# An adaLN block with dilated local attention and a token mixer on one core: modulation rows from four column groups, norm statistics on either engine, the gate folded into the mixer, and a new order of operations

## The chip, the cores and the metric

The kernel runs on one NeuronCore of a Trainium2 chip. Five engines work from instruction queues of their own, each in order: TensorE (PE, matrix products into PSUM), VectorE (DVE), ScalarE (ACT, activation functions and evictions of PSUM), GpSimd (POOL) and SyncE (SP, which issues most transfers). The metric is device microseconds of one execution. A profile has a span of its own, from the first to the last instruction, which is a little shorter than the execution's time.

## The reference

The input x has 2048 tokens of 512 values; everything is bfloat16 outside the sums.

```python
mod = (_silu(c) @ w_mod).reshape(1, 6, 1, -1)
sa, ca, ga, sb, cb, gb = (mod[:, i] for i in range(6))
h = _layernorm(x) * (1 + ca) + sa
x = x + ga * A(h)          # 32 heads of 16; key offsets 0, 2, ... 14
h = _layernorm(x) * (1 + cb) + sb
x = x + gb * B(h)

def A(h):                  # dilated local attention
    q, k, v = split(h @ wqkv)
    logits = q . k[pos - off] * 16 ** -0.5, masked where pos < off
    return (softmax(logits) @ v[pos - off]) @ wo

def B(h):                  # mixes tokens, not channels
    h = _layernorm(h)
    u = gelu(einsum('bsd,sf->bdf', h, w1) + b1)     # f = 1792
    return transpose(einsum('bdf,fs->bds', u, w2) + b2)
```

The gate `ga` scales columns of `wo`; `gb` scales columns (channels) of the mixer's result; `b2` belongs to a token, `b1` to a hidden unit f.

## The kernel before

All 16 token tiles of 128 rows stay in `xx` on chip. The attention runs in four chunks of 512 tokens. For each chunk: the statistics of the first norm (`ln1s`, one per tile, by `bn`, L340: a `bn_stats` and a `bn_aggr` on DVE), the reciprocal deviation (`rstd`, L346: on ACT an Ln and then an Exp with scale -0.5), the negated mean (`negmean`, L352), the norm itself (`ln1n`, L356, on either engine), transposes through PE (`tr`), the scale and shift while these are evicted (`hT`, L529), and q, k, v (`qkv`, L560, evicted by `evq`, `evk`, `evv`). Shifted copies of v are made by 16 transfers per chunk (`vd`, L595).

The logits are four products on DVE (`qk`, 128x4096) summed over channels by column-tiled matmuls (`red`); `max` on DVE and `sub` on PE subtract the maximum, `exp` on ACT makes the weights, `sum` on PE adds them, `rb` (L645) takes on ACT the Ln of the sum and the Exp of its negative, `smul` on DVE scales, `a2` and `a2ev` spread the weights, four products `pv` on DVE and `pvacc` on PE make the output, evicted into `o_sb` by `oev` (L691). `wo` (L707) projects it and adds x by an identity matmul. `x1ev` (L709) evicts the new x with its sum, and `x1sq` (L712) takes the sum of squares on ACT. `mv2` (L721) turns both into the variance on DVE; `rstd2`, `nb2`, the norm `t`, the scale and shift by rows on DVE (`aff`), statistics `ln3s`, `rstd3`, `nb3` and the norm `h3` give the mixer's input.

The mixer's first product (`mlp1`, L786) runs over tokens in two levels, tiles 0 to 7 and 8 to 15. A name such as `mlp1_0_31_4` gives the level, the block of 256 hidden units and its half, and the tile at which four matmuls of 512 columns begin. Level 0 is parked in `gT` (`park`), level 1 is added to it (`gadd`, DVE) and passed through `gelu` (ACT). The second product (`mlp2`, L847) makes 16 output tiles of 14 matmuls; `fin` (L854) adds `b2`, multiplies by the gate row `gb_bc` and adds x, in two DVE passes of 128x512; `st_out` stores. The last tile is done in two halves.

The six modulation vectors come from `sc`, the SiLU of c. Two of them are wanted as columns (`modcols`). The other four are wanted as rows on all 128 partitions: `mod_row` (L469) spreads `sc` into 128 equal columns, multiplies by 512 columns of `w_mod` in four matmuls, and evicts the row to `ga_bc`, `sb_bc`, `ab_bc` or `gb_bc`. `gmul` scales `wo` by `ga_bc`.

Each operation is an entry of a graph with its reads and writes. Nothing schedules them: `schedule` (L139) takes the text `ORDER` (L27 to L76) word by word and emits each operation there; a digit after a colon gives its PSUM slot (four slots of two banks), a letter its engine where there are two. Each engine's queue is the order of its operations in that text. SP's transfers stand in the same text and wait in their own queue. `_EngProxy.wrapped` (L174) records every operation, so that the profile shows nearly everything under L175, and groups are told apart by their tiles.

One word of `ORDER` is `act_table` (L407): it loads a set of activation tables on ACT by its number, 6. In the text of before it is the fourth word.

Of the kernel before, what the change touches and what calls it, by code (L numbers as in the profile page):

```python
# [27 lines left out]
consts ld_x00 consts2 act_table ld_c ld_w0 ld_x02 ld_x2 ld_wmodA ld_wmodB ln1s1 cps:0 warm:1 ld_b2 silu_exp ln1s0  # L28
ld_wmod5 halo0 ld_b1 rstd1_0_0 ld_x1 ln1s3 ld_w1 nb1_0_0 ln1s2 ln1n0:a silu_dve ln1n1:a ld_wo2 sc_rep rstd1_0_2 ln1s9
nb1_0_2 ln1s8 ld_x3 ln1n3:v ln1n2:v ln1s11 ld_w2 modcols:2 ln1s10 tr0_10:3 tr0_12 modcols_cp ld_wmod2 rstd1_2_0  # L30
biascols:0 tr0_00:1 hT0_2 tr0_02 biascols_cp modrow5:2 hT0_0 hT0_3 hT0_1 gb:a qkvq0_1:0 ld_wo3 ln1s5 ld_wmod3
qkvq0_0:3 ln1s6 evq0_1:a qkvk0_1:1 ln1s7 evq0_0:a ld_w1_0_3 ln1s4 qkvq0_2:2 evk0_1:a qk0_1 rstd1_1_0 qkvk0_0:0
evq0_2:a qkvk0_2:3 evk0_0:a nb1_1_0 ln1n6:v ln1n7:a ld_wo0 qk0_0 ld_wo1 ln1n4:a qkvv0_0:1 ld_wmod4 ln1n5:a evk0_2:a
ln1s13 tr1_10:2 evv0_0:a tr1_00:0 ln1s12 red0_0:3 hT1_0:a ln1s14 red0_1 khalo1:a qkvv0_2:1 hT1_2:a qk0_3 hT1_3:a
hT1_1:a modrow2:2 evv0_2:a ln1s15 qkvk1_0:0 ga:a vd0_100 qk0_2 vhalo1:a rstd1_3_0 vd0_011 vd0_110 qkvq1_0:1 evk1_0:a
vd0_001 vd0_101 gmul vd0_031 red0_2 evq1_0:a vd0_131 red0_3 nb1_3_0 nb1_2_0 ln1n10:v vd0_000 qkvk1_2:2 ln1n8:a max0
vd0_030 ln1n9:a vd0_010 qk1_0 ln1n11:a vd0_020 qkvq1_2:0 vd0_111 evk1_2:a vd0_121 khalo2:a vd0_130 tr2_10:1 qk1_1
# [15 lines left out]
mlp1_0_31_0 h3_4:a mlp1_0_01_0 qk3_2 h3_5:a vd3_111 vd3_121 mlp1_0_31_4 vd3_131 mlp1_0_00_4 vd3_101 qk3_3 vd3_031
mlp1_0_11_4 mlp1_0_01_4 mlp1_0_10_4 pv2_0 park0_0:a red3_2 park0_1:a red3_3 mlp1_0_30_4 max3 vd3_120 pvacc2_0:0
vd3_110 park0_3:a pvacc2_1 vd3_130 pv2_2 sub3 oev2_1:a vd3_100 mlp1_0_60_0:1 ld_w1_1_5 exp3 mlp1_0_60_4 ld_w1_1_0
pv2_3 sum3 mlp1_0_61_0 rb3 ld_w1_1_4 mlp1_0_61_4 smul3 pvacc2_2:3 park0_6:a a2_3_0:0 ld_w2_4 a2_3_1 pvacc2_3 a2ev3:a
mlp1_0_20_0:2 oev2_3:a pv3_0 mlp1_0_20_4 wo11:1 ld_w1_1_1 wo8:0 pv3_1 x1ev11 x1sq11 pvacc3_0:3 x1ev8 ld_w2_0 wo9:1
x1sq8 pv3_2 pvacc3_1 x1ev9 wo10:0 oev3_1:a mlp1_0_21_0 pv3_3 x1ev10 ld_w1_1_3 mlp1_0_21_4 x1sq10 x1sq9 pvacc3_2:1
ld_w1_1_2 mv2_2_0 pvacc3_3 park0_2:v rstd2_2_0 mlp1_0_40_0:3 oev3_3:a nb2_2_0 mlp1_0_40_4 t8:v ld_w2_3 t11:a t10:v
t9:v wo12:0 aff2_0 wo14:2 x1ev12 x1sq12 wo15:1 ld_w2_6 x1ev14 ln3s2_3 wo13:0 x1sq14 ln3s2_2 x1ev15 mlp1_0_50_0:2  # L60
ln3s2_0 x1ev13 x1sq15 mlp1_0_51_0 ln3s2_1 x1sq13 ld_w2_7 mlp1_0_51_4 mv2_3_2 rstd3_2_0 mv2_3_0 rstd2_3_2 mlp1_0_50_4
nb3_2_0 h3_11:v h3_9:a nb2_3_2 h3_10:v mlp1_0_41_0 t15:v rstd2_3_0 t14:v h3_8:a nb2_3_0 aff3_2 mlp1_0_41_4 t13:a
mlp1_1_00_0:1 ld_w1_1_6 t12:a ln3s3_3 mlp1_1_01_0 park0_5:a aff3_0 ld_w2_1 mlp1_1_40_0:0 park0_4:a mlp1_1_41_0 ln3s3_0
mlp1_1_30_0:2 ln3s3_1 mlp1_1_31_0 ln3s3_2 rstd3_3_0 ld_w2_2 mlp1_1_10_0:3 nb3_3_0 rstd3_3_2 h3_12:v nb3_3_2 h3_13:a
mlp1_1_11_0 h3_14:v h3_15:v mlp1_1_10_4 mlp1_1_31_4 ld_w2_5 mlp1_1_00_4 mlp1_1_40_4 mlp1_1_11_4 mlp1_1_41_4 gadd1
mlp1_1_01_4 gelu3 mlp1_1_20_0:3 gadd0 gelu2 mlp1_1_20_4 gelu0 mlp1_1_21_0 gelu1 mlp1_1_21_4 mlp1_1_30_4 gadd2
mlp1_1_50_0:1 gadd3 gelu5 mlp1_1_51_0 gelu4 mlp1_1_51_4 gelu7 gadd4 mlp1_1_50_4 gelu6 gelu8 mlp1_1_60_0:3 gadd5
# [155 lines left out]
def kernel(  # L223
# [14 lines left out]
    WARM: int = 15,  # L238
# [28 lines left out]
    def bank(s_, h):  # L267
        return ps[s_.i][:, h, :]
# [37 lines left out]
    gb_bc = T([P, D], F32, "gb_bc")  # L306
# [19 lines left out]
    va2 = small([P, TPC], "va2")  # L326
# [13 lines left out]
    def bn(src, s6, mvt, reads, writes, name):  # L340
        def f():
            nc.vector.bn_stats(s6, src)
            nc.vector.bn_aggr(mvt, s6)
        add("dve", 0.82, f, reads=reads, writes=writes, name=name, lat=0.08)

    def rstd(var_ap, lv_t, rs_t, reads, writes, name):  # L346
        def f():
            nc.scalar.activation(lv_t, var_ap, ACT.Ln, bias=epscol[:, 0:1])
            nc.scalar.activation(rs_t, lv_t, ACT.Exp, scale=-0.5)
        add("act", 0.5, f, reads=list(reads) + ["consts"], writes=writes, name=name, lat=0.05)  # L350

# [545 lines left out]
```

## Time and profile before

| | |
|---|---|
| median of 3 executions (lowest, highest) | 209.24 us (209.02, 209.30) |
| the profiled execution's own time | 209.11 us |
| its span | 207.4 us |
| mean granted TensorE clock | 0.99 |
| instructions | 3356 |
| accumulating activations on ACT | 16 into `xx`, 16 into `junk` |
| statistics on DVE (`BATCH_NORM_STATS2`) | 32, 0.67 us each |
| table loads on ACT | 2, 1.28 us each |

The page gives busy time per engine and, in its chain, the work that ended last, followed back from the end. A timeline row has its start, its duration, the engine, the operation, and output and input by the program's tile names. Neighbouring instructions of one engine overlap by about a tenth of a microsecond, so the distance between starts is what one of them costs in a full queue. `lv` is the result of the Ln of `rstd`, `rs` that of its Exp; `lns` and `rb` are the same for the softmax; `ee` is the softmax's exponential; `junk` takes the unused output of a pass that is run for its sum.

### The profile page before, as it was taken

The numbers are of one execution on the slowest core, as the hardware profiler recorded it, in microseconds if no ns is written. First come the engines' busy times: TensorE is split into PE (matmuls) and PEld (weight loads), VectorE is DVE, ScalarE is ACT, GpSimd is POOL, SyncE is SP. The second block draws the span as 40 slices with busy tenths as digits, with TensorE's granted clock in tenths as the row PEclk, the third lists the DMA queues.
The fourth block names the chain that finished last, engine by engine and source line by source line (L and its number), as shares of the span: only waits on it lengthen the run. The fifth ranks groups of instructions, "written<-read, shape, count | busy, mean of one in ns | idle before, by whom it ended". The sixth has DMA issues, their size and how long they took to land.

```text
span 207.4 us, 3356 instructions
## 1 busy us (share of the span) xinstructions
PE 196.4 (95%) x1290; PEld 91.4 (44%) x1290; DVE 158.4 (76%) x211; ACT 118.9 (57%) x220; POOL 4.0 (2%) x27
## 2 busy tenths in 40 slices
PE   5489999999999999999999999999999999999993
PEld 2155544444454445443353344444444444444452
DVE  2878999999999999999987998954544534543553
ACT  2436998989799999985567979752562000000000
POOL 7000000000000000000000000000000000000000
PEclk9969999999999999999999999999999999999999
DMA  6999939995690496099499999999000111011011
GB/s 185 361 326 319 259 99 179 170 222 128 159 157 4 118 253 150 6 254 259 126 211 290 291 293 292 290 290 250 4 0 0 54 51 48 28 51 51 28 51 51
DMA packets 41571, 32.96 MB, mean 159 GB/s; under 512 B 2004, under 2 KB 38996, under 8 KB 41556
## 3 DMA queue, kind: packets, MB, share of 16 engines
q1 hardware_dynamic: 41548, 32.75, 64.1%
q8 instruction: 10, 0.16, 0.4%
q14 instruction: 5, 0.04, 0.1%
q10 hardware_dynamic: 8, 0.00, 0.0%
HBM read 22.03 MB, written 2.10 MB: 116 GB/s over the span
## 4 chain that ended last, share of the span: by engine, by line
PE 74%; ACT 11%; DMA 6%; DVE 4%; issue 3%; ACTq 0%; SPq 0%; DVEq 0%
PE ps L175 74%; DMA b_t<-in_B_b_dram 4%; ACT h L175 2%; DMA w_q<-in_A_wqkv_dram 2%; ACT hTb L175 1%; ACT v_c L175 1%; ACT junk L175 1%; DVE h L175 1%; DVE st L175 1%; ACT xx L175 1%; ACT n_sb L175 1%; DVE n_sb L175 1%; ACT o_sb L175 0%; ACT a2sb L175 0%; ACT q_sb L175 0%
## 5 line engine op out<-in xcount | busy, mean ns | idle before, releaser
L175 DVE TENSOR_TENSOR pvb<-a2sb,vD 128x4096 bf16<-128x4096 bf16 x16 | 35.9, 2288 | 1.9 <-ACT a2sb L175 1.8
L175 DVE TENSOR_TENSOR prod<-q_sb,k_c 128x4096 bf16<-128x4096 bf16 x16 | 36.2, 2282 | 0.8 <-ACT k_c L175 0.8
L175 PE MATMUL ps<-h,wst 128*128 128x512 bf16 x128 | 29.6, 379 | 0.4 <-ACT h L175 0.3
L175 PEld LDWEIGHTS <-wst 128*128 128x128 bf16 x128 | 12.2, 98 | 16.5 <-issue 2.7
L175 PE MATMUL ps<-gT,vD 128*128 128x512 bf16 x84 | 18.3, 379 | 0.0
L175 PE MATMUL ps<-woq,o_sb 128*128 128x512 bf16 x64 | 16.5, 380 | 0.0
L175 DVE SCALAR_TENSOR_TENSOR q_sb<-ps,b2col,gb_bc 128x512 f32<-128x512 f32 x8 | 6.0, 751 | 12.9 <-PE ps L175 12.9
L175 PEld LDWEIGHTS <-vD 128*128 128x128 bf16 x116 | 9.2, 97 | 14.2 <-DMA vD<-in_w_mod_dram 4.3
L175 PE MATMUL ps<-hTb,w_q 128*128 128x512 bf16 x64 | 15.2, 380 | 0.2 <-ACT hTb L175 0.2
L175 PE MATMUL ps<-hTb,w_k 128*128 128x512 bf16 x64 | 15.2, 380 | 0.0
L175 PE MATMUL ps<-hTb,w_v 128*128 128x512 bf16 x64 | 15.1, 379 | 0.0
L175 PEld LDWEIGHTS <-w_q 128*128 128x128 bf16 x96 | 10.2, 109 | 11.1 <-issue 1.7
L175 DVE SCALAR_TENSOR_TENSOR k_c<-ps,b2col,gb_bc 128x512 f32<-128x512 f32 (+1 forms) x9 | 6.2, 692 | 11.4 <-PE ps L175 11.4
L175 PEld LDWEIGHTS <-o_sb 128*128 128x128 bf16 x106 | 10.0, 98 | 10.5 <-issue 1.7
L175 DVE BATCH_NORM_STATS2 st<-xx 128x6 f32<-128x512 bf16 x16 | 10.8, 676 | 4.4 <-DMA xx<-in_A_x_dram 4.4
L175 PEld LDWEIGHTS <-w_k 128*128 128x128 bf16 x80 | 8.7, 111 | 8.9 <-issue 0.8
L175 PE MATMUL ps<-gT,prod 128*128 128x512 bf16 x56 | 12.4, 379 | 0.1
L175 PE MATMUL ps<-gT,pvb 128*128 128x512 bf16 x56 | 12.2, 379 | 0.0
L175 PEld LDWEIGHTS <-w_v 128*128 128x128 bf16 x80 | 8.6, 110 | 7.9 <-issue 0.4
L175 ACT ACTIVATE xx<-ps 128x512 bf16<-128x512 f32 x16 | 9.4, 586 | 2.7 <-PE ps L175 2.5
L175 DVE BATCH_NORM_STATS2 st<-h 128x6 f32<-128x512 bf16 x16 | 10.8, 674 | 0.1
L175 ACT ACTIVATE hTb<-ps,sacol,a1col 128x512 bf16<-128x512 bf16 x14 | 10.6, 787 | 0.0
(100 smaller groups left out, 286.5 us busy)
## 6 DMA issues: line engine op xcount, KB each, us to landing
vD<-v_c SPq DMA_DIRECT2D x64, 131.5 KB, 4.5
wst<-in_B_w_dram SPq DMA_DIRECT2D x8, 512.0 KB, 7.1
vD<-in_B_w_dram SPq DMA_DIRECT2D x3, 896.0 KB, 9.1
wst<-in_w_mod_dram SPq DMA_DIRECT2D x4, 512.0 KB, 8.7
prod<-in_B_w_dram SPq DMA_DIRECT2D x2, 896.0 KB, 8.9
pvb<-in_B_w_dram SPq DMA_DIRECT2D x2, 896.0 KB, 10.0
xx<-in_A_x_dram SPq DMA_DIRECT2D x3, 512.0 KB, 7.2
vD<-in_w_mod_dram SPq DMA_DIRECT2D x2, 512.0 KB, 7.2
```

The source lines that it names most:

```text
L175: r = fn(*a, **k)
```

## The change

- The four modulation rows come from one operation, `modrows`: `sc` is spread into 32 columns, and each of the four rows is made in one 32-column group of PE, 16 matmuls in all, in one PSUM bank. One eviction (`mrow_ev`) adds 1 to the third row by a column `onecol`, and four transfers (`bc0` to `bc3`) read one row of each group and spread it over 128 partitions.
- `bn` becomes `stats`: on DVE as before, or on ACT by two accumulating passes (the mean, and the sum of squares about it). Sixteen of the 32 statistics are placed on ACT (nine of the first norm, seven of the third). `rstd` takes a scale for its Ln, since ACT's form is 512 times the variance; where statistics of both kinds stand in one group, the Ln is issued once for each run of one kind.
- `x1sq` takes squares about the mean, so that `mv2` goes.
- The gate `gb` is multiplied into `gT` after each Gelu (`gbm`, DVE). `xb` computes `gb * b2 + x` ahead for each output tile, and `fin` is one addition.
- `ORDER` is new as a whole: other engines for norms and evictions, PSUM slots, places of transfers. The warm-up of 15 matmuls is five batches of 8, 4, 3, 3 and 3. The first tiles of x load as 2, 1 and 1. `act_table` stands after `pv3_3`.

The diff, cut to its core; of `ORDER` only the lines with `act_table` are shown:

```diff
-consts ld_x00 consts2 act_table ld_c ld_w0 ld_x02 ld_x2 ld_wmodA ld_wmodB ln1s1 cps:0 warm:1 ld_b2 silu_exp ln1s0
+consts consts2 ld_x02 ld_c warm1:0 ld_x00 ld_wmodA ld_x01 warm4:1 ld_wmodB ld_w1 ln1s2:v ln1s3:a cps:2 warm0:3 ld_x1
...
+x1ev8 ld_w1_1_5 pv3_3 act_table mlp1_0_21_0 x1sq8 rstd2_2_0 mlp1_0_21_4 oev3_1:a pvacc3_2:1 nb2_2_0 ld_w2_3 t8:v t10:a
+pvacc3_3 t9:v mlp1_0_50_0:0 t11:v oev3_3:a aff2_0 wo12:3 ld_w1_1_4 wo13:1 x1ev12 ln3s2_3:v x1sq12 wo15:3 ln3s2_0:v
...
-    WARM: int = 15,
+    WARM=(8, 4, 3, 3, 3),
...
-    def bn(src, s6, mvt, reads, writes, name):
-        def f():
+    def stats(src, s6, mvt, reads, writes, name):
+        def f_dve():
             nc.vector.bn_stats(s6, src)
             nc.vector.bn_aggr(mvt, s6)
-        add("dve", 0.82, f, reads=reads, writes=writes, name=name, lat=0.08)
-
-    def rstd(var_ap, lv_t, rs_t, reads, writes, name):
+
+        def f_act():
+            nc.scalar.activation(junk[:], src, ACT.Identity, scale=1.0 / D, accum_out=mvt[:, 0:1])
+            nc.scalar.activation(junk[:], src, ACT.Square, scale=-1.0, bias=mvt[:, 0:1], accum_out=mvt[:, 1:2])
+        return G.add_any([("dve", 0.82, f_dve), ("act", 1.24, f_act)], reads=reads, writes=writes, name=name, lat=0.08)
+
+    def rstd(var_ap, lv_t, rs_t, reads, writes, name, scales):
         def f():
-            nc.scalar.activation(lv_t, var_ap, ACT.Ln, bias=epscol[:, 0:1])
+            sc_ = [x() for x in scales]
+            i0 = 0
+            for i in range(1, len(sc_) + 1):
+                if i == len(sc_) or sc_[i] != sc_[i0]:
+                    nc.scalar.activation(lv_t[:, i0:i], var_ap[:, i0:i], ACT.Ln, scale=sc_[i0], bias=epscol[:, 0:1])
+                    i0 = i
             nc.scalar.activation(rs_t, lv_t, ACT.Exp, scale=-0.5)
...
+        def f_mm():
+            for kt in range(KT):
+                for r in range(4):
+                    nc.tensor.matmul(bank(sr, 0)[32 * r:32 * r + 32, :], lhsT=sc_rep[:, kt, :], rhs=wblk[r][:, kt, :],
+                                     start=(kt == 0), stop=(kt == KT - 1), tile_position=(0, 32 * r))
...
+        for r, (t_, key) in enumerate(((ga_bc, "ga_bc"), (sb_bc, "sb_bc"), (ab_bc, "ab_bc"), (gb_bc, "gb_bc"))):
+            row = mrow[32 * r:32 * r + 32, :]
+            src = bass.AP(row.tensor, row.offset, [list(row.ap[0]), [0, 4], [1, D]])
+            dma(t_[:], src, P * D * 2, ["mrow"], [key], f"bc{r}")
...
             add("act", _act(D, 0, False) + 0.22, lambda sl=sl, st=st: nc.scalar.activation(
-                junk[:], xx[:, st, :], ACT.Square, scale=float(D) ** -0.5, accum_out=sq2[b][:, sl:sl + 1]),
-                reads=[("xx", st)], writes=[("sq2", b, sl)], name=f"x1sq{st}", lat=0.1)
+                junk[:], xx[:, st, :], ACT.Square, scale=-float(D), bias=su2[b][:, sl:sl + 1],
...
+                    add("dve", 0.34, lambda ft=ft, fl=fl: nc.vector.tensor_tensor(
+                        gT[:, ft + fl, :], gT[:, ft + fl, :], gb_bc[:], op=ALU.mult),
...
+            add("dve", _tt1(D), lambda st=st, otmp=otmp: nc.vector.scalar_tensor_tensor(
+                otmp, gb_bc[:], b2col[:, st:st + 1], xx[:, st, :], op0=ALU.mult, op1=ALU.add),
...
-                    nc.vector.scalar_tensor_tensor(otmp[:, c0:c1], bank(sf, 0)[:, 0:c1 - c0], b2col[:, st:st + 1],
-                                                   gb_bc[:, c0:c1], op0=ALU.add, op1=ALU.mult)
-                    nc.vector.tensor_tensor(ostage[:, c0:c1], otmp[:, c0:c1], xx[:, st, c0:c1], op=ALU.add)
...
+                add("dve", _tt1(nc_), lambda st=st, sf=sf, otmp=otmp, ostage=ostage, c0=c0, c1=c1: nc.vector.tensor_tensor(
+                    ostage[:, c0:c1], bank(sf, 0)[:, 0:c1 - c0], otmp[:, c0:c1], op=ALU.add),
```

More of the change, by code (lines that the diff above doesn't have):

```diff
@@ L33 @@
[L33 to L37, printed above, removed]
@@ L53 @@
[L53 to L57, printed above, removed]
@@ L58 @@
[L58 to L67, printed above, removed]
@@ new lines @@
+ld_wmod3 evq1_0:a vd0_100 vd0_021 ln1s13:a vd0_030 vhalo1:v qk1_0 sub0 vd0_000 qkvq1_2:3 vd0_001 exp0 vd0_130 evk1_2:a
+vd0_020 qk1_1 sum0 ld_wo3 evq1_2:a red1_0:2 vd0_121 tr2_10:0 rb0 vd0_131 qkvv1_0:3 hT2_2:a smul0 vd0_111 hT2_3:a qk1_2
+vd0_110 a2_0_0:1 evv1_0:a a2_0_1 red1_1 tr2_00:0 a2ev0:a qkvv1_2:3 qk1_3 hT2_0:a ln1s14:a red1_2 pv0_0 modrows:1
+hT2_1:a evv1_2:a red1_3 qkvk2_0:0 ln1s12:a vd0_101 vd1_001 max1 vd1_021 rstd1_3_0 pvacc0_0:3 pv0_1 mrow_ev sub1
+evk2_0:a bc0 qkvq2_0:1 exp1 vd1_020 nb1_3_0 pv0_2 ld_wo1 ln1n15:a sum1 vd1_000 qkvk2_2:0 evq2_0:a vd1_011 vd1_030 rb1
@@ new lines @@
+ln1n14:v khalo2:a vd1_010 ln1n13:a pvacc0_1 ln1n12:v ld_b2 smul1 qkvq2_2:1 evk2_2:a vd1_120 pv0_3 vd1_031 oev0_1:a
+vd1_100 tr3_00:2 evq2_2:a vd1_130 a2_1_0:0 a2_1_1 vd1_131 gmul pvacc0_2:3 a2ev1:a vd1_110 pvacc0_3 tr3_10:1 vd1_101
+vhalo2:v oev0_3:a pv1_0 qkvv2_2:0 vd1_121 bc2 hT3_0:a ld_b1 hT3_2:a vd1_111 wo2:3 khalo3:a hT3_1:a pv1_1 ld_w1_0_3
+hT3_3:a bc1 wo0:2 x1ev2 evv2_2:a wo1:1 qk2_1 x1ev0 pvacc1_0:3 x1ev1 pvacc1_1 wo3:0 x1sq1 pv1_2 x1sq2 qkvv2_0:2 x1ev3
+x1sq0 x1sq3 pv1_3 qkvk3_0:1 oev1_1:a rstd2_0_0 evv2_0:a pvacc1_2:0 nb2_0_0 t2:v pvacc1_3 t3:v t1:a qkvq3_0:3 vd2_021
@@ new lines @@
+mlp1_0_30_0:1 vd2_030 ln3s1_0:a ld_w1_0_5 qk3_0 mlp1_0_31_0 vd2_000 ln3s1_2:a a2_2_1 ld_w1_0_4 mlp1_0_00_0:0 qk3_1
+a2ev2:a mlp1_0_01_0 rstd3_1_0 mlp1_0_60_0:3 evv3_0:a mlp1_0_61_0 nb3_1_0 h3_6:v h3_7:a h3_5:v red3_0:2 pv2_1 h3_4:a
+red3_1 vhalo3:a mlp1_0_00_4 vd3_030 vd3_011 mlp1_0_31_4 qk3_2 vd2_010 vd3_031 mlp1_0_60_4 vd3_000 mlp1_0_01_4 vd3_010
+qk3_3 vd3_021 mlp1_0_61_4 vd3_020 mlp1_0_30_4 vd2_101 park0_6:a vd3_131 red3_2 park0_0:a pv2_0 red3_3 mlp1_0_40_0:3
+park0_3:a mlp1_0_40_4 max3 vd3_110 pvacc2_0:0 vd3_130 pvacc2_1 pv2_2 mlp1_0_10_0:1 vd3_001 vd3_100 sub3 vd3_120
@@ new lines @@
+mlp1_0_11_0 exp3 pv2_3 mlp1_0_11_4 oev2_1:a sum3 mlp1_0_10_4 rb3 pvacc2_2:0 smul3 ld_w1_1_1 pvacc2_3 vd3_101 a2_3_0:2
+a2_3_1 oev2_3:v vd3_111 mlp1_0_41_0 a2ev3:a vd3_121 mlp1_0_41_4 ld_w1_1_0 pv3_0 ld_w1_1_3 wo11:0 park0_4:a wo9:2
+park0_1:a pv3_1 x1ev11 pvacc3_0:3 x1ev9 wo10:1 ld_w2_4 x1sq11 x1sq9 pv3_2 wo8:0 x1ev10 pvacc3_1 x1sq10 mlp1_0_20_0:2
+x1ev8 ld_w1_1_5 pv3_3 act_table mlp1_0_21_0 x1sq8 rstd2_2_0 mlp1_0_21_4 oev3_1:a pvacc3_2:1 nb2_2_0 ld_w2_3 t8:v t10:a
+pvacc3_3 t9:v mlp1_0_50_0:0 t11:v oev3_3:a aff2_0 wo12:3 ld_w1_1_4 wo13:1 x1ev12 ln3s2_3:v x1sq12 wo15:3 ln3s2_0:v
@@ L76 @@
+mlp2_15_0_256:1 fin15_0 st_out15_0 st_out14_0 mlp2_15_12_256 fin15_256 st_out15_256
 """
@@ L423, with f_warm @@
     add("dve", 0.5, f_silu2, reads=[sl_c, "ecol"], writes=["sc", "ecol"], name="silu_dve", use=[sl_c])
-    sl_m, sl_w = G.slot("ps"), G.slot("ps")
-    def f_warm():
-        for i in range(WARM):
-            nc.tensor.matmul(bank(sl_w, i % 2), lhsT=ident[:], rhs=ident[:].unsqueeze(1).to_broadcast([P, 4, P]),
-                             start=True, stop=True)
-    add("pe", 0.43 * 8 + 0.216 * (WARM - 8), f_warm, reads=["consts"], writes=[sl_w], name="warm", use=[sl_w])
+    sl_m = G.slot("ps")
+    for wi, wn in enumerate(WARM):
+        sl_w = G.slot("ps")
+        def f_warm(wn=wn, sl_w=sl_w):
+            for i in range(wn):
+                nc.tensor.matmul(bank(sl_w, i % 2), lhsT=ident[:], rhs=ident[:].unsqueeze(1).to_broadcast([P, 4, P]),
+                                 start=True, stop=True)
+        add("pe", 0.216 * wn, f_warm, reads=["consts"], writes=[sl_w], name=f"warm{wi}", use=[sl_w])
     def f_cols():
@@ L448, in build_bias @@
     def build_bias():
-        load(b1_t[:], B_b1.rearrange("(t p) -> t p", p=P), F * 2, [], ["b1_t"], "ld_b1")
-        load(b2_t[:], B_b2.rearrange("(t p) -> t p", p=P), S * 2, [], ["b2_t"], "ld_b2")
+        dma(b1_t[:], B_b1.rearrange("(t p) -> t p", p=P), F * 2, [], ["b1_t"], "ld_b1")
+        dma(b2_t[:], B_b2.rearrange("(t p) -> t p", p=P), S * 2, [], ["b2_t"], "ld_b2")
         sb_ = G.slot("ps")
@@ L464, in build_mod_rows @@
     def build_mod_rows():
-        sc_rep = gT[:, 0, :].rearrange("p (k m) -> p k m", k=KT)
-        add("dve", 0.34, lambda: nc.vector.tensor_copy(sc_rep, sc[:].unsqueeze(2).to_broadcast([P, KT, P])),
+        sc_rep = gT[:, 0, 0:KT * 32].rearrange("p (k m) -> p k m", k=KT)
+        add("dve", 0.15, lambda: nc.vector.tensor_copy(sc_rep, sc[:].unsqueeze(2).to_broadcast([P, KT, 32])),
             reads=["sc"], writes=[("gT", 0)], name="sc_rep", lat=0.1)
-        def mod_row(idx, consume, cname, cwrites):
-            slot = idx - 2
-            wblk = wst[slot][:].rearrange("p a b -> p (a b)").rearrange("p (k n) -> p k n", k=KT)
-            load(wblk, wmod_view[:, :, idx * D:(idx + 1) * D], D * D * 2, [], [("wst", slot)], f"ld_wmod{idx}")
-            sr = G.slot("ps")
-            def f_mm():
-                for kt in range(KT):
-                    nc.tensor.matmul(bank(sr, 0), lhsT=sc_rep[:, kt, :], rhs=wblk[:, kt, :],
-                                     start=(kt == 0), stop=(kt == KT - 1))
-            add("pe", _mm(512, 4), f_mm, reads=[("gT", 0), ("wst", slot)], writes=[sr], name=f"modrow{idx}", lat=0.2,
-                use=[sr])
-            G.add_any([("act", _act(D), lambda: nc.scalar.activation(consume, bank(sr, 0), ACT.Identity,
-                                                                     bias=1.0 if cname == "ab" else 0.0)),
-                       ("dve", 0.62, lambda: nc.vector.tensor_scalar_add(consume, bank(sr, 0), 1.0) if cname == "ab"
-                        else nc.vector.tensor_copy(consume, bank(sr, 0)))],
-                      reads=[sr], writes=cwrites, name=cname, lat=0.1, use=[sr])
@@ L487, in build_mod_rows @@
-        mod_row(2, ga_bc[:], "ga", ["ga_bc"])
+        wblk = []
+        for slot in range(4):
+            idx = slot + 2
+            wblk.append(wst[slot][:].rearrange("p a b -> p (a b)").rearrange("p (k n) -> p k n", k=KT))
+            dma(wblk[slot], wmod_view[:, :, idx * D:(idx + 1) * D], D * D * 2, [], [("wst", slot)], f"ld_wmod{idx}")
+        sr = G.slot("ps")
+        def f_mm():
[3 more added lines that the diff above has]
+                                     start=(kt == 0), stop=(kt == KT - 1), tile_position=(0, 32 * r))
@@ new lines, in build_mod_rows @@
+        add("pe", 16 * 0.054, f_mm, reads=[("gT", 0)] + [("wst", r) for r in range(4)], writes=[sr], name="modrows",
+            lat=0.2, use=[sr])
+        add("act", _act(D), lambda: nc.scalar.activation(mrow[:], bank(sr, 0), ACT.Identity, bias=onecol[:, 0:1]),
+            reads=[sr, "consts"], writes=["mrow"], name="mrow_ev", lat=0.1, use=[sr])
+        for r, (t_, key) in enumerate(((ga_bc, "ga_bc"), (sb_bc, "sb_bc"), (ab_bc, "ab_bc"), (gb_bc, "gb_bc"))):
+            row = mrow[32 * r:32 * r + 32, :]
+            src = bass.AP(row.tensor, row.offset, [list(row.ap[0]), [0, 4], [1, D]])
+            dma(t_[:], src, P * D * 2, ["mrow"], [key], f"bc{r}")
@@ L508, in build_chunk @@
             rk, nk = ("rs0", b, g0), ("nb0", b, g0)
-            rstd(mv[0][b][:, g0:g1, 1], lv[0][b][:, g0:g1], rs[0][b][:, g0:g1], ks, [rk], f"rstd1_{ch}_{g0}")
+            rstd(mv[0][b][:, g0:g1, 1], lv[0][b][:, g0:g1], rs[0][b][:, g0:g1], ks, [rk], f"rstd1_{ch}_{g0}",
+                 [stat_scale(o) for o in sts[g0:g1]])
             negmean(nb[0][b][:, g0:g1], mv[0][b][:, g0:g1, 0], rs[0][b][:, g0:g1], ks + [rk], [nk], f"nb1_{ch}_{g0}")
@@ L740, in build_chunk @@
             add("dve", 2 * _tt2(n * D), f, reads=hk + ["ab_bc", "sb_bc"], writes=hk, name=f"aff{ch}_{g0}", lat=0.08)
-            for sl in range(g0, g1):
-                bn(h2[b][:, sl, :], st6[1][b][:, sl, :], mv[1][b][:, sl, :], [("h2", b, sl)], [("mv1", b, sl)],
-                   f"ln3s{ch}_{sl}")
+            sts = [stats(h2[b][:, sl, :], st6[1][b][:, sl, :], mv[1][b][:, sl, :], [("h2", b, sl)], [("mv1", b, sl)],
+                         f"ln3s{ch}_{sl}") for sl in range(g0, g1)]
             ks = [("mv1", b, sl) for sl in range(g0, g1)]
             rk, nk = ("rs2", b, g0), ("nb2", b, g0)
-            rstd(mv[1][b][:, g0:g1, 1], lv[2][b][:, g0:g1], rs[2][b][:, g0:g1], ks, [rk], f"rstd3_{ch}_{g0}")
+            rstd(mv[1][b][:, g0:g1, 1], lv[2][b][:, g0:g1], rs[2][b][:, g0:g1], ks, [rk], f"rstd3_{ch}_{g0}",
+                 [stat_scale(o) for o in sts])
             negmean(nb[2][b][:, g0:g1], mv[1][b][:, g0:g1, 0], rs[2][b][:, g0:g1], ks + [rk], [nk], f"nb3_{ch}_{g0}")
```

109 lines of the change are left out of this document (54 added, 55 removed).

## The prediction

> **What bounds the kernel now.** I read part 1 of the page first, then the chain of waits in order of time. (Chain: start, us, what; part 1: busy us, share, instructions.)
>
> ```profile
> PE 196.4 (95%) x1290; PEld 91.4 (44%) x1290; DVE 158.4 (76%) x211; ACT 118.9 (57%) x220; POOL 4.0 (2%) x27
> ```
> ```profile
> 12.86 29.76 PE ps L175 x194
> ...
> 96.31 58.81 PE ps L175 x361
> ...
> 157.84 45.97 PE ps L175 x226
> 203.81 0.03 issue
> 203.83 0.49 DVE k_c L175
> ```
> TensorE (PE) bounds it: three long stretches hold 134.5 of 207.4 us. Between 43 and 97 us pieces of ACT and DVE alternate with PE. ScalarE (ACT) looks idle (57%), but that is a mean: the windows give it 9.63, 9.90 and 9.90 us of ten at 60-70, 70-80 and 80-90 us. It evicts PSUM for PE and its queue is in order, so I read next what one place in that queue costs (ACT timeline: start, duration, instruction; overlapping neighbours mean that the distance between starts counts).
>
> ```profile
> 0.80 1.28 ACT L175 ACT_TABLE_LOAD   x1 [0.80 <-PEq L881]
> ...
> 2.43 0.17 ACT L175 ACTIVATE ecol<-ps 128x4 f32<-128x4 f32 x1 [0.35 <-PE ps L175]
> ```
> ```profile
> 63.06 0.63 ACT L175 ACTIVATE junk<-xx 128x512 bf16<-128x512 bf16 x1
> 63.60 0.19 ACT L175 ACTIVATION_READ_ACCUMULATOR junk<-xx 128x1 f32 x1
> 63.69 0.58 ACT L175 ACTIVATE xx<-ps 128x512 bf16<-128x512 f32 x1
> 64.17 0.19 ACT L175 ACTIVATION_READ_ACCUMULATOR xx<-ps 128x1 f32 x1
> 64.39 0.63 ACT L175 ACTIVATE junk<-xx 128x512 bf16<-128x512 bf16 x1
> ...
> 85.50 0.29 ACT L175 ACTIVATE lv<-mv,epscol 128x4 f32<-128x4 f32 x1
> 85.83 0.21 ACT L175 ACTIVATE rs<-lv 128x4 f32<-128x4 f32 x1
> 85.94 1.01 ACT L175 ACTIVATE v_c<-ps 128x1024 bf16<-128x1024 f32 x1
> 86.84 0.27 ACT L175 ACTIVATE lns<-ps 128x128 f32<-128x128 f32 x1
> 87.15 0.31 ACT L175 ACTIVATE rb<-lns 128x128 bf16<-128x128 f32 x1
> 87.36 2.92 ACT L175 ACTIVATE h<-h,nb,rs 128x512 bf16<-128x512 bf16 x4
> ```
> ```profile
> 119.75 1.01 ACT L175 ACTIVATE o_sb<-ps 128x1024 bf16<-128x1024 f32 x1
> ...
> 136.66 0.80 ACT L175 ACTIVATE h<-h,nb,rs 128x512 bf16<-128x512 bf16 x1
> 137.47 1.28 ACT L175 ACT_TABLE_LOAD   x1
> ```
> Ln then Exp takes 0.33 + 0.11 us (85.50, 85.83, 85.94), the softmax pair 0.31 + 0.2, an eviction of 1024 columns 0.91, a normalisation 0.71, a 512-column pass with an accumulator 0.63 to 0.72 (I use 0.68; 0.66 for the eviction into xx). A table load takes 1.28 and starts only when its predecessor has wholly ended (136.66 + 0.80), so it also loses the usual 0.1 of overlap. The kernel has two: at 0.80, which serves every Ln and Exp, and before the Gelus.
>
> **The table loads.** The token `act_table`, fourth in the old order, stands after `pv3_3` in the new one. The built program therefore holds 29 table loads on ACT instead of 2:
>
> ```
> 41 LoadActFuncSet
> 42 Activation lv_0_130<-mv_0_126,epscol 128x3
> 43 Activation lv_0_130<-mv_0_126,epscol 128x1
> 44 LoadActFuncSet
> 45 Activation rs_0_136<-lv_0_130 128x4
> ```
> Ln gets one set (number 5), Exp another (0), and the old set (6, both functions) returns only at the late `act_table`. Nine `rstd` and all four `rb` stand before it: 13 x 2 = 26 loads, with the first, the explicit and the Gelu load 29. One pair costs 2 x (1.28 + 0.1) = 2.8 us, in the queue and in the latency behind it.
>
> **ACT's queue up to one common point.** I take the last eviction of o_sb (`oev3_3`, the row at 119.75, ended 120.7); `wo12` to `wo15`, chunk 3's norms and the rest of the mixer stand behind it. The new queue holds up to there, count x distance: 28 loads 35.9; 40 accumulating passes (12 `x1sq`, 14 statistics of two passes) 27.2; 42 passes of 1024 columns out of PSUM 38.4; 13 normalisations 9.2; 12 hT (0.67, from neighbours at 46.54 and 47.21) 8.0; 12 evictions into xx 7.9; 17 Ln and 10 Exp 6.7; softmax pairs 2.0; small ones 2.2. Sum 137.7, without loads 101.8. The old queue, counted alike, is 92.9, without its load 91.6. So 10.2 us come from statistics less the norms handed to DVE: the 27 us that ACT then idled before 120.7 would cover that. The 35 of the loads are not covered.
>
> **Waits on top.** Overlap lost at 27 loads: 2.7. Start: the first x is there at 3.6 (DVE's first row), the first pair ends at 8.5, the second at 12.8, `hT0` begins at 14.9 behind transposes that need its norms, the third pair ends at 22.9, the first v eviction at 23.9; its queue sum with lost overlap is 19.8, so 4.1 of waiting. From 24 to 125 I find ACT always supplied: DVE and PE wait for it behind nearly every pair (about 36, 48, 60, 67, 86, 102, 107, 113, 123). Loops where it waits: `park0_6` stands behind five mixer units (4 x 0.215 = 0.86 each) that only start when `h3_4` is out (125.2), so 4.4; `exp3` waits for four 2.2 us products and a 1.14 us reduction on DVE, then `sub3`, 3.1; `a2ev3` for `smul3` and 32 small matmuls, 1.7; crumbs 1.8, together 11.0. Bounds: 0, if DVE and PE get that far ahead, and 11 as the walk gives; I take 11. The eviction ends at 137.7 + 2.7 + 4.1 + 11.0 = 155.5, 34.8 later than now.
>
> **What PE still has then.** From `wo12` on 372 matmuls of 512 columns (before: 384 from the same point; more of the mixer can run early). The old rate: `wo12` started at 121.27, the last matmul ended at 203.81, 82.5 / 384 = 0.215 each. 12 fewer: -2.6.
>
> **The rest.** `gbm`: 14 multiplies of 128x512 on DVE, 0.36 each (half the distance of the 128x1024 rows); 12 lie beside 24 us of mixer matmuls, the last two follow the last Gelus in the place where PE waited on DVE and ACT (155 to 157.8): +0.45. Other handovers of chunk 3: +1.0 (0 to 3). `fin` keeps one pass, `xb` is computed earlier, on a DVE that works 1.4 of every 3 us there; of the final 0.48 + 0.42 the second goes: -0.4. `modrows`: 16 matmuls in four column groups at about 61 ns (`red`: 16 in 0.98 us) replace 16 of 0.213: 2.4 us of PE, now at a time when PE waits for ACT: 0 (-2.4 without that cover). `bc0` to `bc3`: four transfers of 128 KB like the v copies (4.5 us to landing); `ga_bc` lands near 66, `gmul` runs at 70: 0; they join SP's queue between v copies, where about 0.4 us of issue each is covered. The later `ld_b1`, `ld_b2`, `ld_wo1`, and the split `ld_x00`: 0 (b1 is wanted at the Gelus). `ld_w2_5` now stands on SP behind `st_out0`, but lands in 10 us and is wanted by the eleventh output tile, 30 us on; `st_out5`, moved back past two tiles, holds only the fourth next one: 0, and 0.5 each if wrong. Five warm batches, 21 matmuls for 15, fill waits at the start: 0; if exposed, 6 x 0.213 = +1.3. The variance without `mv2`: two DVE instructions of 0.15 less per group, on an engine that waits: 0, at most -1.
>
> PE's clock: granted 0.56, 0.50, 0.50 and 0.73 in the four windows from 12 to 16 us, after the idle at 8 to 12, so 1.7 us of PE time lost. In the walk PE waits over 2.5 us about eight times, so 0 to 13; on ACT's path stands only the wait of 5 us before the mixer units at 125: I take 1.5.
>
> Sum: 207.4 + 34.8 - 2.6 + 0.45 + 1.0 - 0.4 + 1.5 = 242.2 us of span. The profiled execution took 209.11 for its 207.4, so 1.7 around it; the median, 209.24, is 0.1 above it: 244.0.
>
> The Trainium skill, "ScalarE: Activation LUTs", section What ACT_TABLE_LOAD costs, gives 1283 ns for the load, as both rows here, and a drain of about 1380 ns with every switch. The rows speak against the drain: at 137.47 the load begins the moment its predecessor ends, and at 0.80 + 1.28 = 2.08 no 1.38 follows, since `ecol` runs at 2.43.
>
> **Rivals.** (1) ACT absorbs every later wait: 244.0 - 11.0 - 1.5 = 231.5. For it: DVE and PE have some 35 us of slack. Against: the loops named need ACT, DVE and PE in turn. (2) A switch costs twice what the rows show, by a drain that no row here could show between two live sets: 27 x 1.28 = 34.6 more, 279. This is the skill's rule above; the two rows speak against it.
> (3) Faster: the loads do not run as built, because the set that held both functions is kept. Then ACT has only its extra 10.2 us against 27 idle, `oev3_3` is set by PE again, and 209.2 - 2.4 (`modrows`) - 0.4 (end) + 0.45 (`gbm`) - 2 (start: no `modrow5`, 1.9 at 13.8, before the first qkv) = 205. It decides once fewer than six of the 13 pairs are left, 6 x 2.8 being the idle that remains. For: one load serves all pairs now. Against: the late Gelu load was put in at the build too, and it ran.
> The same page, section Table sets: the hidden batching unit, says Ln followed by Exp needs one load, as one set holds both; by that rule it would be rival 3, but the built program alternates sets 5 and 0.
>
> **How the numbers follow.** Forecast 0.72 (own range 236 to 256, the top from the clock's bound), rival 1 0.16, rival 2 0.05, rival 3 0.06, no change 0.01. The range, 231 to 256, leaves out rivals 2 and 3 and the edges. A difference under 0.2% cannot be told from none: faster 0.06, same 0.01, slower 0.93.
>
> **What would show it.** 29 table loads near 1.28 us, ACT busy near 160 us and 9 tenths or more from 20 to 120 us; the last o_sb eviction near 155 and about 84 us from its end to the end of the span; PE's share near 80%, with waits on rs and rb; PE unbroken after 165. Wrong if the loads are fewer, if starts lie over 2.5 us behind a load's start, or if PE's clock stays halved for tens of us.

## The result, and the profile after

The changed kernel takes 244.53 us (median of 4 executions, 243.63 to 246.48), the kernel before 209.27 (209.02 to 209.35): a ratio of 1.170, with a 95% interval of 1.1628 to 1.1771. The profiled execution took 244.39 us for a span of 242.7.

Part 1 of the page after (busy us, share of the span, instructions) and its costliest group:

```profile
PE 204.3 (84%) x1275; PEld 93.9 (39%) x1296; DVE 157.1 (65%) x203; ACT 164.1 (68%) x296; POOL 4.2 (2%) x29
...
L176 ACT ACT_TABLE_LOAD x29 | 37.2, 1283 | 1.9 <-PEq L895 1.4
```

TensorE fell from 95% of the span to 84%, ScalarE rose from 118.9 to 164.1 us, and 37.2 us of ScalarE's time are 29 table loads of 1.283 us. By the means ScalarE still looks free for a third of the time. From 20 to 120 us it is busy for 97.9 of 100 us (before: 85.7).

ScalarE's timeline after (start, us, engine, line, operation; in brackets the idle time before it and what ended it) shows a pair of loads at the start, and further down the waits and the last eviction of `o_sb`:

```profile
5.14 0.19 ACT L176 ACTIVATION_READ_ACCUMULATOR junk<-xx,mv 128x1 f32 x1
5.34 1.28 ACT L176 ACT_TABLE_LOAD   x1
6.64 0.48 ACT L176 ACTIVATE lv<-mv,epscol 128x1 f32<-128x1 f32 x2
7.14 1.28 ACT L176 ACT_TABLE_LOAD   x1
8.43 0.20 ACT L176 ACTIVATE rs<-lv 128x2 f32<-128x2 f32 x1
...
130.10 2.85 ACT L176 ACTIVATE gT<-ps 128x1024 bf16<-128x1024 f32 x3 [4.42 <-remote]
136.15 1.02 ACT L176 ACTIVATE ee<-ps 128x1024 bf16<-128x1024 f32 x1 [3.19 <-PE ps L176]
...
142.76 1.02 ACT L176 ACTIVATE a2sb<-ps 128x1024 bf16<-128x1024 f32 x1 [1.46 <-PE ps L176]
145.54 1.94 ACT L176 ACTIVATE gT<-ps 128x1024 bf16<-128x1024 f32 x2 [1.76 <-PE ps L176]
...
156.87 1.01 ACT L176 ACTIVATE o_sb<-ps 128x1024 bf16<-128x1024 f32 x1
```

In the rows of before, the Exp of `rstd` began 0.33 us after its Ln (85.50, 85.83). Here Ln and Exp each stand behind a load, and from the end of the statistics (5.14 + 0.19 = 5.33) to the Exp at 8.43 it takes 3.1 us. A load begins when its predecessor has ended, and the next function starts 1.29 to 1.30 us after the load did. The last eviction of `o_sb` ends at 157.88; before it was 120.76.

Who waits for ScalarE is read in the view of waits (engine, tile <- releaser: us in total, times, longest):

```profile
DVE nb L176 <- ACT rs L176: 28.3, 12, 3.6
...
DVE ee L176 <- ACT rb L176: 12.4, 4, 4.8
```

VectorE stands 40.7 us behind the two operations that hold the loads: `rstd` and `rb`. Before, the same view has 0.2 us for `rs` and no row for `rb`. And the chain of waits (start, us, what), near the end of the attention and from the last Gelu on:

```profile
138.11 1.28 ACT L176
139.40 0.28 ACT lns L176
139.70 1.28 ACT L176
140.99 0.32 ACT rb L176
141.34 0.70 DVE ee L176
142.08 0.63 PE ps L176 x32
142.87 5.53 PE ps L176 x17
148.43 0.69 ACT xx L176 x2
...
193.11 0.44 DVE gT L176
193.59 3.18 PE ps L176 x14
196.82 10.74 PE ps L176 x49
...
239.58 0.42 DVE k_c L176
```

The loads stand on the path themselves (138.11 and 139.70, the nameless ScalarE pieces), with what they delay: `rb` on ScalarE, `ee` on VectorE, then TensorE. The chain's shares are ScalarE 48% and TensorE 34%. From 193.59 on TensorE sets the end alone, as it did before from 157.84.

### The profile page after: what moved, and what is told of

It reads as the page before. It is cut to its first block, busy times and chain, and to the rows that moved or that the text cites. A ratio compares the mean times of both kernels' runs of the same rounds, so it can differ in the third digit from the quotient of the medians.

```text
span 242.7 us, 3409 instructions
## 1 busy us (share of the span) xinstructions
PE 204.3 (84%) x1275; PEld 93.9 (39%) x1296; DVE 157.1 (65%) x203; ACT 164.1 (68%) x296; POOL 4.2 (2%) x29
## 4 chain that ended last, share of the span: by engine, by line
ACT 48%; PE 34%; DVE 6%; SPq 4%; issue 4%; DMA 3%; ACTq 0%
PE ps L176 34%; ACT junk L176 13%; ACT L176 11%; SPq L176 4%; ACT xx L176 3%; ACT v_c L176 3%; ACT lv L176 2%; ACT hTb L176 2%; ACT h L176 2%; ACT k_c L176 2%; DVE h L176 2%; ACT q_sb L176 2%; DMA b_t<-in_B_b_dram 2%; ACT o_sb L176 2%; DVE n_sb L176 1%
## 5 line engine op out<-in xcount | busy, mean ns | idle before, releaser
L176 ACT ACT_TABLE_LOAD x29 | 37.2, 1283 | 1.9 <-PEq L895 1.4
L176 DVE TENSOR_TENSOR pvb<-a2sb,vD 128x4096 bf16<-128x4096 bf16 x16 | 36.4, 2288 | 2.6 <-PE ps L176 1.4
L176 PE MATMUL ps<-woq,o_sb 128*128 128x512 bf16 x63 | 17.5, 394 | 3.5 <-ACT o_sb L176 2.0
L176 PE MATMUL ps<-hTb,w_q 128*128 128x512 bf16 x62 | 16.2, 402 | 3.3 <-ACT mrow L176 3.2
L176 PE MATMUL ps<-hTb,w_v 128*128 128x512 bf16 x59 | 17.5, 434 | 0.7 <-ACT a2sb L176 0.2
L176 DVE TENSOR_TENSOR k_c<-ps,k_c 128x512 bf16<-128x512 f32 (+1 forms) x9 | 5.6, 631 | 18.6 <-PE ps L176 18.6
L176 PEld LDWEIGHTS <-o_sb 128*128 128x128 bf16 x106 | 10.1, 100 | 15.5 <-issue 4.6
L176 DVE SCALAR_TENSOR_TENSOR nb<-mv,rs 128x4 f32<-128x4 f32 (+1 forms) x10 | 1.6, 162 | 20.4 <-ACT rs L176 20.4
L176 PEld LDWEIGHTS <-ident 128*128 128x128 bf16 (+1 forms) x79 | 8.2, 119 | 16.1 <-issue 11.6
L176 PEld LDWEIGHTS <-w_v 128*128 128x128 bf16 x80 | 9.2, 117 | 12.4 <-issue 6.5
L176 PE MATMUL ps<-prod,group 128*32 128x512 bf16 x128 | 9.1, 382 | 5.2 <-DVE prod L176 2.9
L176 ACT ACTIVATE junk<-xx,su 128x512 bf16<-128x512 bf16 x16 | 11.5, 719 | 0.3
```

The lines of the kernel that those rows point to most:

```text
L176: r = fn(*a, **k)
```

## The experiments

Every experiment starts from one of the two kernels. "The table-first kernel" is the changed kernel with nothing but the word `act_table` moved.

**1. The changed kernel with the table load early.**

```diff
-consts consts2 ld_x02 ld_c warm1:0 ld_x00
+consts consts2 ld_x02 ld_c act_table warm1:0 ld_x00
...
-x1ev8 ld_w1_1_5 pv3_3 act_table mlp1_0_21_0 x1sq8
+x1ev8 ld_w1_1_5 pv3_3 mlp1_0_21_0 x1sq8
```

> The changed kernel with the word act_table moved from behind pv3_3 to behind ld_c; the built program then has 2 table loads instead of 29, and every other queue is the same. Theory (the loads are the whole loss): about 205 us as in rival 3, between 202 and 208, ratio to the kernel before 0.965 to 0.995. Rival (statistics on ACT, the gate's multiplies and the new order cost as well): 215 us or more.

It took 208.30 us (207.66 to 209.85, 12 executions), a ratio of 0.9981 (0.995 to 1.0012): with two loads instead of 29 it is 36.2 us faster than the changed kernel, and the whole slowdown is gone. The rest of the change together makes no difference that can be told: the time lies just above the 202 to 208 us of the theory, which also expected some 4 us of gain from the rest. Its ScalarE timeline, at the places of the waits shown above:

```profile
99.13 2.85 ACT L176 ACTIVATE gT<-ps 128x1024 bf16<-128x1024 f32 x3 [4.42 <-PE ps L176]
105.18 1.02 ACT L176 ACTIVATE ee<-ps 128x1024 bf16<-128x1024 f32 x1 [3.20 <-PE ps L176]
...
109.66 1.02 ACT L176 ACTIVATE a2sb<-ps 128x1024 bf16<-128x1024 f32 x1 [1.68 <-PE ps L176]
111.48 1.94 ACT L176 ACTIVATE gT<-ps 128x1024 bf16<-128x1024 f32 x2 [0.80 <-PE ps L176]
```

The same three waits are here without the loads, 4.42, 3.20 and 1.68 us long. They belong to the new order, and the loads shift them without filling them: what ScalarE waits for there is itself made from what ScalarE put out late. Where the gain of the rest went is seen in TensorE's timeline of the table-first kernel:

```profile
80.42 0.59 PE L176 MATMUL ps<-nm,ident 128*128 128x512 bf16 x2 [0.87 <-DVE nm L176]
83.69 0.61 PE L176 MATMUL ps<-ee,ident 128*128 128x128 bf16 x8 [0.95 <-ACT ee L176]
91.69 1.89 PE L176 MATMUL ps<-h,w_v 128*128 128x512 bf16 x8 [1.25 <-ACT a2sb L176]
```

Its first q, k, v product starts at 12.18 us, before at 15.54. But TensorE then idles 5.4 us between 20 and 160 us, against 1.3 before, 3.4 of it from 70 to 100 us, and the long stretch at the end of the chain begins at 157.76 us, before at 157.84. ScalarE is busy for 68.9 of the 70 us from 20 to 90 us: with the 16 statistics it is full even without the loads.

**2. Loads that switch nothing.** The table-first kernel, with a load of the set that is already there ahead of each Ln and each Exp of the first 13 pairs, so that ScalarE's queue is that of the changed kernel less one load.

```diff
+    def more_loads():
+        if n_more[0] < 26:
+            n_more[0] += 1
+            nc.scalar.add_instruction(mybir.InstLoadActFuncSet(
+                name=nc.get_next_instruction_name(), act_func_set_id=6, ins=[], outs=[]))
```

> The changed kernel with act_table behind ld_c, and with 26 further loads of the same set 6 put before the first Ln and the Exp of the first 13 pairs, so that ACT's queue is the changed kernel's but for one load, and no set ever changes. Theory (a load costs its place in ACT's queue, whichever set it brings): 243 to 245 us, one load below the changed kernel. Rival (a switch to another set costs more than a load, by a drain or otherwise): clearly under that, by up to 27 x 1.38 = 37 us if it were the full drain; rival (loads of a set that is already there are skipped): 205 us.

242.55 us (242.05 to 243.33, 4 executions), ratio 1.1594 (1.1542 to 1.1645). Its ScalarE timeline at the first pair:

```profile
5.13 1.28 ACT L176 ACT_TABLE_LOAD   x1
6.43 0.48 ACT L176 ACTIVATE lv<-mv,epscol 128x1 f32<-128x1 f32 x2
6.93 1.28 ACT L176 ACT_TABLE_LOAD   x1
8.22 0.20 ACT L176 ACTIVATE rs<-lv 128x2 f32<-128x2 f32 x1
```

The distances are those of the changed kernel to 0.01 us, and the time is just under the 243 to 245 us of the theory. The 2.0 us between the two medians is near the one load that this kernel has less (1.38 by the count), the rest lies within the spread of the changed kernel's runs. A real switch costs no more than a load of the set that is in use, and the time is the load instruction's own.

**3. The table load in the middle.** `act_table` stands behind `rb0`, so that five of the 13 pairs are left and eight become plain.

```diff
-tr2_10:0 rb0 vd0_131 qkvv1_0:3
+tr2_10:0 rb0 act_table vd0_131 qkvv1_0:3
```

> The changed kernel with act_table behind rb0: five pairs of loads are left (13 loads in the program). On record stands that fewer than six pairs would be covered by ACT's idle time: no slower than 209. Strictly additive, 2.8 us a pair: 205 + 14 = 219. A third reading, that the first three pairs lie in the start, where x, the norms, the transposes and q, k, v follow one another and nothing covers them: about 205 + 3 x 2.8 + 1 to 2 = 214 to 216.

222.87 us (222.68 to 223.11, 4 executions), ratio 1.065 (1.0606 to 1.0695), with 13 loads. The five early pairs and `act_table` itself, 11 loads more than in the table-first kernel, cost 222.87 - 208.30 = 14.6 us, 1.32 a load; the eight later pairs, 16 loads, 244.53 - 222.87 = 21.7, 1.35 a load. A load costs nearly its 1.38 us in both halves of the order, and the five pairs that one reading had as covered are not free. None of the three expected times came. The additive one was nearest: counted from the measured 208.30 and with `act_table` as a load of its own, it is 208.30 + 11 x 1.38 = 223.5 us.

**4. All statistics on VectorE.** The table-first kernel with the letter of the 16 `ln1s` and `ln3s` on ScalarE changed.

```diff
-ln1s3:a
+ln1s3:v
...
-ln3s1_0:a
+ln3s1_0:v
```

> The changed kernel with act_table behind ld_c, and with all 32 statistics on DVE, where the order has 16 on ACT. If both engines have room: within 1 us of the run with act_table first alone. If DVE, which was 9.6 to 10 of 10 us busy between 40 and 100 us before the change, is the limit, 16 x 0.8 = 12.8 us more work there: up to 12 us slower than that run. If ACT is the limit, faster than it by up to 16 x 0.6 = 10.

217.47 us (215.21 to 217.86, 6 executions), ratio 1.0373 (1.0324 to 1.0422). That is within the up to 12 us of the reading in which VectorE is the limit. In the view of waits ScalarE now waits for the statistics (1.6 us in the table-first kernel):

```profile
ACT lv L176 <- DVE mv L176: 19.2, 6, 5.5
```

So in the new order the 16 statistics on ScalarE are worth 9.2 us, although they fill it.

**5. The late load in the old order.** The kernel before, with `act_table` moved behind `pv3_3` and nothing else.

```diff
-consts ld_x00 consts2 act_table ld_c ld_w0
+consts ld_x00 consts2 ld_c ld_w0
...
-wo10:0 oev3_1:a mlp1_0_21_0 pv3_3 x1ev10
+wo10:0 oev3_1:a mlp1_0_21_0 pv3_3 act_table x1ev10
```

> The kernel before, with nothing changed but the word act_table moved from the fourth place to behind pv3_3: 29 table loads, 13 pairs of them before that point. Theory as it stands after the first four runs (a pair costs 2.8 us wherever it stands, ACT's idle time covers none): 209.3 + 13 x 2.8 = 245. Rival, as in the prediction's reading of the old queue (92.9 us of work up to the last o_sb eviction, some 27 us of idle time before it, which partly covers the loads): 228 to 237. Rival (the late loads hurt only a queue that also carries 16 statistics): under 220.

237.03 us (236.65 to 238.84, 4 executions), ratio 1.1335 (1.1287 to 1.1383), with 29 loads: 27.4 us more than the 209.62 us of the kernel before, measured beside it. The theory's 245 us did not come; the time stands at the upper end of the first rival. The same loads cost 8.8 us less than in the new order, so the old order did cover some of them.

**6. The late load and all statistics on VectorE.** The changed kernel with experiment 4's edit, to tell whether the statistics or the order took the cover away.

```diff
-ln1s3:a
+ln1s3:v
...
-ln3s1_0:a
+ln3s1_0:v
```

> The changed kernel with all 32 statistics on DVE and the table load where the change put it, so 29 loads. The loads cost 36.2 us where 16 statistics were on ACT (244.5 against 208.3) and 27.5 us in the old order, which has its statistics on DVE (237.0 against 209.5). Theory: ACT's queue lost the idle time that could cover loads to the statistics alone; with them on DVE the cost over the same kernel with one load (217.5) falls to that of the old order or below: 217.5 + 27.5 = 245 or less. Rival: the new order as such leaves ACT no idle time where the loads stand, wherever the statistics are; then 217.5 + 36.2 = 253.7.

242.27 us (239.32 to 245.23, 4 executions), ratio 1.1589 (1.149 to 1.1687), with 28 loads, so 26 more than in experiment 4 (the 29th of the changed kernel stands ahead of its first statistic on ScalarE, which is not there now). Over that kernel's 217.47 they cost 24.8 us (21.5 to 30.0 between the extremes of the two kernels): the theory held. Set beside ScalarE's idle time from 20 to 120 us in the same kernels without the added loads (its windows), and counting 1.38 us a load:

| kernel without the loads | idle, us | loads added | their time | cost measured | covered |
|---|---|---|---|---|---|
| before | 14.2 | 27 | 37.3 | 27.4 | 9.9 |
| table-first | 11.6 | 27 | 37.3 | 36.2 | 1.1 |
| table-first, statistics on VectorE | 34.1 | 26 | 35.9 | 24.8 | 11.1 |

The last row's cover is uncertain by the same extremes, 5.9 to 14.4 us. Idle time covers loads only in part, and in the table-first kernel next to nothing: 10.1 of its 11.6 us are the four waits of experiment 1, which move with the loads.

**7. The gate not folded.** The table-first kernel without `gbm` and `xb`, `fin` in two passes as before.

```diff
-                    add("dve", 0.34, lambda ft=ft, fl=fl: nc.vector.tensor_tensor(
-                        gT[:, ft + fl, :], gT[:, ft + fl, :], gb_bc[:], op=ALU.mult),
-                        reads=[("gT", ft + fl), "gb_bc"], writes=[("gT", ft + fl)], name=f"gbm{ft + fl}", lat=0.1)
...
+                    nc.vector.scalar_tensor_tensor(otmp[:, c0:c1], bank(sf, 0)[:, 0:c1 - c0], b2col[:, st:st + 1],
+                                                   gb_bc[:, c0:c1], op0=ALU.add, op1=ALU.mult)
+                    nc.vector.tensor_tensor(ostage[:, c0:c1], otmp[:, c0:c1], xx[:, st, c0:c1], op=ALU.add)
```

> The changed kernel with act_table behind ld_c and with the gate taken out of the mixer again: no gbm, no xb, fin in two passes. By the terms of the prediction: the last two multiplies behind the last Gelus gone, -0.45, the second pass at the very end back, +0.4: within 0.5 us of 208.3. Rival (the multiplies also crowd DVE among the additions and Gelus of level 1): 1 to 3 us faster than 208.3. Rival (fin in two passes holds PSUM slots too long): 1 to 3 us slower.

209.44 us (207.85 to 210.15, 12 executions), ratio 0.998 (0.9951 to 1.0009), the same as the table-first kernel's 0.9981 (the kernel before took 209.62 us beside this one, 209.39 beside that): the fold is worth nothing that 12 executions can tell.

**8 and 9. Work moved off the full ScalarE.** The table-first kernel with `ln3s1_0` on VectorE; and one with `h3_7` and `h3_4` there too, both ahead of `pv2_1`.

```diff
-mlp1_0_30_0:1 vd2_030 ln3s1_0:a ld_w1_0_5
+mlp1_0_30_0:1 vd2_030 ln3s1_0:v ld_w1_0_5
```

> The changed kernel with act_table behind ld_c and one statistic (ln3s1_0) moved from ACT to DVE. In the run with the table first, ACT ran 98% from 20 to 95 us and PE waited 1.25 us for a2ev2 behind three statistics. If ACT sets the time there: 0.7 to 1.4 us faster than 208.3. If DVE does: up to 0.8 us slower. If both are level: no difference.

> As the run with one statistic moved, and with the norms h3_4 and h3_7 on DVE as well (0.35 us each there, 0.71 on ACT): ACT 2.8 us shorter between 85 and 95 us, DVE 1.5 us longer. If ACT alone sets the time of the mixer's units that wait for h3_4: 1.5 to 2.5 us faster than 208.3. If DVE is level with it: 0 to 1 us slower, through pv2_1, which then starts later.

208.94 us (207.32 to 209.75), ratio 0.9962 (0.9936 to 0.9987), and 209.51 us (208.47 to 210.0), ratio 0.9985 (0.9961 to 1.0009), 12 executions each. The gains expected if ScalarE alone set the time, 0.7 to 1.4 and 1.5 to 2.5 us, did not come; both results fit the reading in which VectorE is level with it, which nothing here shows directly. The first is the only version whose interval leaves 1 out, by 0.4% on the mean; it isn't told apart from the table-first kernel (0.995 to 1.0012), so that it beats the kernel before rests on this one interval.

## Why the prediction was right

The forecast was 244.0 us, and the median is 244.53. Its steps one by one:

- **29 loads of 1.28 us, 2.8 us a pair, uncovered.** Shown: 29 loads of 1.283 us; 2.6 to 2.7 us a pair in both halves of the order (experiment 3); 36.2 us from the one word (experiment 1), for which the forecast's queue sum and lost overlap hold 27 x 1.38 = 37.3.
- **ScalarE's queue to the last `o_sb` eviction.** Forecast 155.5 with the clock's 1.5 us booked apart, though its place lay ahead of that eviction: 157.0. Measured 157.88. Up to there ScalarE was busy for 140.0 us and idle for 17.8, where the forecast had 137.7 + 2.7 = 140.4 of work and 4.1 + 11.0 + 1.5 = 16.6 of waiting. (The terms of the queue as written add up to 137.5, not 137.7; 0.2 us changes nothing.) The first v eviction was forecast to end at 23.9 and ended at 23.8 (22.80 + 1.01).
- **Waits on top.** Forecast 4.4, 3.1 and 1.7 for `park0_6`, `exp3` and `a2ev3`; measured 4.42, 3.19 and 1.46. That 11.0 was taken and not 0 was right for the reason given, loops that go through ScalarE itself: experiment 1 has the same waits with no load in them.
- **TensorE behind it.** 372 matmuls x 0.215 + 0.45 + 1.0 = 81.4; from `wo12` at 157.93 to the last end at 239.55 it took 81.6. The idle rows in it are 0.68 and 0.55 us, the latter behind the last `gbm`; those multiplies took 0.419 us each and not 0.36. "Unbroken after 165" holds but for these two.
- **The end.** The second pass of `fin` is gone, 3.2 us from the last matmul to the end of the span instead of 3.6: -0.4, as forecast. From the eviction to the end 84.8 us were measured and 85.2 forecast.
- **`modrows` and the warm batches at 0.** The 16 matmuls of `modrows` take 1.03 us at 53.22 us, as forecast. That they and the warm batches cost nothing where they stand was argued and not tried alone; TensorE waited 3.2 us for the eviction `mrow_ev`, which stands behind a pair of loads here, and 0.2 in the table-first kernel.

Three steps were wrong, without moving the sum:

- **The clock's place.** "On ACT's path stands only the wait of 5 us before the mixer units at 125": there the granted clock stayed at 1.00. It fell where TensorE waited for the last `rb`. The windows of the changed kernel (us; TensorE busy, matmuls; granted clock; DMA share; GB/s):

```profile
140.00:141.00 1.00, 0.13 (x4) 1.00 0.41 87
141.00:142.00 1.00, 0.00 (x0) 1.00 0.83 238
142.00:143.00 1.00, 0.76 (x33) 1.00 1.25 389
143.00:144.00 1.00, 1.00 (x4) 0.72 0.97 197
144.00:145.00 1.00, 1.00 (x4) 0.50 1.05 219
145.00:146.00 1.00, 1.00 (x4) 0.50 1.18 282
146.00:147.00 1.00, 1.00 (x4) 0.58 1.20 289
147.00:148.00 1.00, 1.00 (x6) 1.00 1.20 291
```

  (The number in brackets counts a matmul in every window that it touches.) From `w_q` at 142.87 to the second `wo` at 147.15 it takes 4.28 us; in the table-first kernel, at full clock, the same matmuls take 2.82 (109.54 to 112.36). The wait of `park0_4` behind them is 1.76 us, there 0.80, and the second `x1ev` behind that comes another 0.5 us later (148.43, there 113.87). So 1.5 us stand on ScalarE's path: the size that was booked, at a place that the forecast hadn't named, and that is luck. The clock also fell elsewhere, to 0.50 between 11 and 17 us, where `hT0` began at 14.90 as forecast, and to a mean of 0.62 from 100 to 110 us and 0.86 from 110 to 120. In the last two ScalarE was busy for 9.88 and 9.77 of ten us all the same, and TensorE then waited 2.34 us for a norm on VectorE that needs ScalarE's `rs` of 123.02. Slower matmuls count as busy: with the same matmuls TensorE is busy for 194.4 us in the table-first kernel and 204.3 here, and so its share is 84% where the forecast had 80%.
- **Rival 3's point, "fewer than six of the 13 pairs".** Five pairs and `act_table` cost 14.6 us. The rival counted ScalarE's idle time as free room for loads. The forecast itself had found that the waits are loops through ScalarE, and by that finding the room wasn't there: the rival should have been held against it.
- **Rival 3's time, 205.** Measured 208.3 with the loads gone. The start did get shorter and `modrows` is cheaper, but TensorE's idle time between 20 and 160 us grew from 1.3 to 5.4 us, 4.1 more, against 2.4 + 2 counted as gain. The extra 10.2 us were set against 27 idle (25.8 by the windows, from 0 to 120.7 us), a sum over 120 us. The extra work stands where ScalarE had little left, 20 to 90 us, and leaves it 1.1 us of idle time there.

Rival 1 (later waits absorbed, 231.5) fell with the waits measured. Rival 2 (a switch at twice the price, 279) fell with the distances of 1.29 to 1.30 us and with experiment 2. Rival 3 itself (the loads don't run as built) fell with the 29 loads in the trace. The Trainium skill, "ScalarE: Activation LUTs", section What ACT_TABLE_LOAD costs, gives a drain of about 1380 ns with every switch on top of the load: no row here shows it, neither for a switch nor for a load of the same set. The same page's section Table sets: the hidden batching unit says that Ln followed by Exp needs one load, as one set holds both. That holds in experiment 1, where set 6 was loaded ahead of them, and not in the changed kernel, where each of the 13 pairs has two loads.

## What to carry to other kernels

Count the table loads in the built program, not in the source: here one word of the order decides between 2 and 29, and it alone costs 36.2 us, all of the slowdown of 35.3. When an engine's queue gets longer, don't set the addition against that engine's idle time as a sum: look at each wait that makes up the idle time, and where it ends by work that came from the same engine, it moves along and covers nothing. And read the busy share by stage: at 57% on the mean, ScalarE had not a tenth left between 60 and 90 us.

## What was not expected of the hardware

- A load of a table set that is already in use takes the same 1.28 us as a switch, and delays the next function by the same 1.30 us (experiment 2).
- The granted clock began to fall between 143 and 144 us, to 0.50 from 144 on, after TensorE had come back from an idle time of 1.95 us (140.13 to 142.08), and was back at 1.00 by 147; by the four windows 1.70 us of TensorE time are lost. After a longer idle time, of 2.34 us up to 124.19 us, it stayed at 1.00. The length of the idle time alone doesn't tell; what does was not tried.
